# An attention backward kernel: K and V also read through a transposing DMA instead of being transposed on TensorE

## The chip, the cores and the metric

The kernel runs on one core of a Trainium2 chip. The metric is device time in microseconds (us), as the median of several executions. Engines are named as in the profile: PE is TensorE, PEld is TensorE loading the operand that a matmul holds still, DVE is VectorE, ACT is ScalarE, POOL is GpSimd, SP is SyncE, which computes nothing here and only issues DMAs. A q behind a name (SPq) is that engine's instruction queue. PSUM is the memory into which matmuls write in these kernels. The granted clock is the share of TensorE's full clock that the trace records: 1 or 0.5 at any moment here.

## The reference, cut to what matters

Two independent attention blocks (A and B) with batch 8, 96 queries, 32 heads, 512 cached keys, head size 128, model width 640, all bfloat16. The program returns the forward output and, for a given output gradient, the gradients of x, K, V, wq and wo:

```python
q = (x @ wq).reshape(B, Sq, H, Dh).transpose(0, 2, 1, 3)
scores = jnp.einsum("bhqd,bhkd->bhqk", q, k_cache) * (Dh ** -0.5)
p = softmax(scores)
o = jnp.einsum("bhqk,bhkd->bhqd", p, v_cache)
out = o.transpose(0, 2, 1, 3).reshape(B, Sq, H * Dh) @ wo      # then jax.vjp of it
```

One (block, head, batch) triple is a *cell*. There are 2 x 32 x 8 = 512 cells. Each needs K and V twice: with keys on the partitions (for dQ and O), as they lie in memory, and with the head dimension on the partitions (for the scores S and for dP), which is their transpose.

## The kernel before

A cell's work is cut into steps that are emitted tick by tick, so that several cells overlap. The parts that the change touches (cuts are marked with `# ...`):

```python
OFF = dict(ld=0, s1=2, s2=3, s3=3, s4=4, s5=5, s6=6, s7=7, s8=8)   # tick of each step

def c_ld(h, b):                       # natural K and V; partition p holds keys 4p..4p+3
    K_sb = kvp.tile([128, KC, 128], BF16, name="K_sb", bufs=11)
    V_sb = kvp.tile([128, KC, 128], BF16, name="V_sb", bufs=8)
    nc.sync.dma_start(K_sb[:], kc[b, h].rearrange("(p c) d -> p c d", c=KC))
    nc.sync.dma_start(V_sb[:], vc[b, h].rearrange("(p c) d -> p c d", c=KC))

def c_s1(h, b):                       # eight PE transposes into one PSUM bank, one DVE copy
    for c in range(KC):
        nc.tensor.transpose(kvT_ps[:, c * 128:(c + 1) * 128], st["K_sb"][:, c, :], ident[:])
    for c in range(KC):
        nc.tensor.transpose(kvT_ps[:, Sk + c * 128:Sk + (c + 1) * 128], st["V_sb"][:, c, :], ident[:])
    nc.vector.tensor_copy(KVT[:], kvT_ps[:])

def c_s2a(h, b):                      # scores: one matmul of 512 moving columns
    nc.tensor.matmul(S_ps[:], hs["QT_h"][:, tok], st["KT"], start=True, stop=True)
# ... softmax; P_sb scaled on POOL; O, dV, dP, dS, dQ ...
def c_s7(h, b):                       # dK: four matmuls, ACT copies out of PSUM, SP stores
    # ...
    dK_sb = wk.tile([128, KC * 128], BF16, name="dK_sb", bufs=3)
    nc.scalar.activation(dK_sb[:], dK_ps[:], ACT.Identity, scale=1.0)
    nc.sync.dma_start(dk[b, h].rearrange("(p c) d -> p (c d)", c=KC), dK_sb[:])
```

dV is stored the same way in step 4. Per head, wo and wq are also transposed on PE (ten transposes). SP issues four copies of 128 KB for each cell: K, V, dK, dV.

## Time and profile before

1850.55 us (median of two runs, 1850.18 to 1850.92).

| resource | busy of 1849 us |
|---|---|
| PE | 1818 (98%) |
| DVE / ACT / POOL | 1519 / 1434 / 778 |
| 16 DMA engines, mean packet time | 1071 (58%) |
| SP: its records plus the short gaps between them | 880 + 130 = 1010 (55%) |

A DMA queue's packet time is summed and divided by 16 engines. For SP, I add the durations of all its instructions and every gap of at most 150 ns between two of them: those short gaps recur after each instruction and are not waits.

From the page of the kernel before: the span, the busy times, the granted clock and DMA share in 40 slices of the span, the two DMA queues that matter (packets, MB, share), the chain that ended last, and two groups of instructions (count, total busy us, mean ns of one, then idle time just before them and what ended most of it):

```profile
span 1848.8 us, 69797 instructions
...
PE 1818.4 (98%) x26595; PEld 1571.4 (85%) x26744; DVE 1518.6 (82%) x3309; ACT 1434.4 (78%) x4041; POOL 777.9 (42%) x1378
...
PEclk9999999999999999999999999999999999999999
DMA  7666654666546655566575665456655566555652
...
q1 hardware_dynamic: 296480, 270.53, 46.2%
q0 software_dynamic: 19872, 60.32, 10.7%
...
PE 95%; POOL 2%; issue 1%; DVE 1%; DMA 1%; ACT 0%; POOLq 0%; SPq 0%; ACTq 0%
...
L396 ACT ACTIVATE dK_sb<-dK_ps 128x512 bf16<-128x512 f32 x512 | 300.5, 587 | 15.7 <-PE dK_ps L394 12.9
...
L259 PE MATMUL S_ps<-KVT,QT_h 128*96 128x512 bf16 x512 | 193.8, 379 | 2.2 <-DVE KVT L247 1.9
```

PE is full, the clock is fully granted, and the chain is 95% PE. The S matmul takes 379 ns and waits for almost nothing (2.2 us in all).

The SP queue in a stretch of the same trace; columns are start, duration, queue, line, operation:

```profile
901.18 0.34 SPq L397 DMA_DIRECT2D out_dram<-dK_sb  x1
902.18 0.34 SPq L333 DMA_DIRECT2D out_dram<-dV_sb  x1
903.09 0.34 SPq L233 DMA_DIRECT2D K_sb<-in_B_k_cache_dram  x1
903.66 1.38 SPq L234 DMA_DIRECT2D V_sb<-in_B_v_cache_dram  x1
```

A copy holds SP for 0.34 us, with free time between.

### The profile page before, as it was taken

The page shows a single profiled execution, that of the slowest core. Times are in us where ns is not written, and L with a number is a line of the kernel's source. Part 1 is how long each engine was busy: PE and PEld are TensorE (multiplying, and loading weights), DVE is VectorE, ACT ScalarE, POOL GpSimd, SP SyncE. Part 2 cuts the span into 40 slices and gives each one's busy share as a digit, 9 for nine tenths or more (in the row PEclk, how much of TensorE's full clock was granted, in tenths as well). Part 3 has the DMA queues.
Part 4 walks back from the last instruction along what each step waited for, and adds up shares of the span by engine and source line. Part 5 has one row for each costly group of instructions (what it writes and reads, how often), then busy time and mean ns, then how long its engine had stood idle before and what let it go on. Part 6 is the DMA issues. An engine that isn't in the chain of part 4 may idle for free.

```text
span 1848.8 us, 69797 instructions
## 1 busy us (share of the span) xinstructions
PE 1818.4 (98%) x26595; PEld 1571.4 (85%) x26744; DVE 1518.6 (82%) x3309; ACT 1434.4 (78%) x4041; POOL 777.9 (42%) x1378
## 2 busy tenths in 40 slices
PE   6999999999999999999999999999999999999998
PEld 5888888888888888888888888888888888888887
DVE  5888867888788887888878887678887888878885
ACT  4888877888668886788767888788876788767882
POOL 4444433444334443345455444334433444333435
PEclk9999999999999999999999999999999999999999
DMA  7666654666546655566575665456655566555652
GB/s 229 196 193 202 192 162 149 199 195 193 164 148 194 201 183 165 159 191 205 186 229 173 196 194 184 160 167 198 192 175 164 171 196 199 159 165 176 201 168 84
DMA packets 316688, 335.32 MB, mean 181 GB/s; under 512 B 38368, under 2 KB 302048, under 8 KB 316352
## 3 DMA queue, kind: packets, MB, share of 16 engines
q1 hardware_dynamic: 296480, 270.53, 46.2%
q0 software_dynamic: 19872, 60.32, 10.7%
q8 instruction: 210, 3.44, 0.8%
q14 instruction: 126, 1.03, 0.2%
HBM read 171.57 MB, written 159.12 MB: 179 GB/s over the span
## 4 chain that ended last, share of the span: by engine, by line
PE 95%; POOL 2%; issue 1%; DVE 1%; DMA 1%; ACT 0%; POOLq 0%; SPq 0%; ACTq 0%
PE q_ps L210 11%; PE o_ps L480 10%; PE dV_ps L330 6%; PE kvT_ps L243 6%; PE kvT_ps L245 6%; PE dK_ps L394 6%; PE dP_ps L352 6%; PE S_ps L259 6%; PE dwq_ps L445 6%; PE dwo_ps L425 5%; PE optp_ps L313 5%; PE dq_dst_ps L377 5%; PE optp_ps L306 5%; PE dq_dst_ps L370 5%; PE n_ps L225 3%; PE nat_ps L410 2%
## 5 line engine op out<-in xcount | busy, mean ns | idle before, releaser
L290 POOL TENSOR_SCALAR P_sb<-E_sb,rinv 96x512 bf16<-96x512 bf16 x512 | 354.2, 692 | 780.5 <-DVE rinv L281 775.2
L271 ACT ACTIVATE E_sb<-S_ps,negm 96x512 bf16<-96x512 f32 x512 | 349.1, 682 | 291.2 <-DVE negm L261 288.1
L356 DVE SCALAR_TENSOR_TENSOR dS_sb<-dP_ps,dl_ps,P_sb 96x512 bf16<-96x512 f32 x512 | 383.3, 749 | 108.1 <-PE dl_ps L354 103.1
L247 DVE COPY KVT<-kvT_ps 128x1024 bf16<-128x1024 bf16 x512 | 350.0, 684 | 70.7 <-PE kvT_ps L245 69.0
L261 DVE TENSOR_REDUCE negm<-S_ps 96x1 f32<-96x512 f32 x512 | 347.6, 679 | 35.8 <-PE S_ps L259 30.1
L332 ACT ACTIVATE dV_sb<-dV_ps 128x512 bf16<-128x512 f32 x512 | 313.3, 612 | 0.0
L396 ACT ACTIVATE dK_sb<-dK_ps 128x512 bf16<-128x512 f32 x512 | 300.5, 587 | 15.7 <-PE dK_ps L394 12.9
L319 ACT ACTIVATE PT_sb<-optp_ps 128x384 bf16<-128x384 bf16 x512 | 253.4, 495 | 0.0
L245 PE MATMUL kvT_ps<-ident,V_sb 128*128 128x128 bf16 x2048 | 198.0, 219 | 0.0
L394 PE MATMUL dK_ps<-Qnat_h,dS_sb 96*128 96x128 bf16 x2048 | 197.9, 219 | 0.0
L243 PE MATMUL kvT_ps<-ident,K_sb 128*128 128x128 bf16 x2048 | 197.9, 219 | 0.0
L330 PE MATMUL dV_ps<-dOnat_h,P_sb 96*128 96x128 bf16 x2048 | 197.9, 219 | 0.0
L259 PE MATMUL S_ps<-KVT,QT_h 128*96 128x512 bf16 x512 | 193.8, 379 | 2.2 <-DVE KVT L247 1.9
L352 PE MATMUL dP_ps<-KVT,dOT_h 128*96 128x512 bf16 x512 | 195.2, 381 | 0.0
L342 POOL TENSOR_TENSOR prod<-OT_h,dOT_h 128x96 bf16<-128x96 bf16 x512 | 186.2, 364 | 19.4 <-ACT OT_h L316 14.4
L243 PEld LDWEIGHTS <-K_sb 128*128 128x128 bf16 x2048 | 147.3, 98 | 36.9 <-issue 1.9
L379 DVE COPY dST_sb<-dq_dst_ps 128x384 bf16<-128x384 bf16 x512 | 175.4, 343 | 1.8 <-PE dq_dst_ps L377 0.8
L313 PE MATMUL optp_ps<-ident,P_sb 96*128 96x96 bf16 x2048 | 171.6, 205 | 2.3 <-POOL P_sb L290 2.0
L377 PE MATMUL dq_dst_ps<-ident,dS_sb 96*128 96x96 bf16 x2048 | 172.1, 206 | 0.5 <-DVE dS_sb L356 0.4
L306 PE MATMUL optp_ps<-PT_sb,V_sb 128*128 128x96 bf16 x2048 | 172.1, 206 | 0.0
L370 PE MATMUL dq_dst_ps<-dST_sb,K_sb 128*128 128x96 bf16 x2048 | 170.7, 206 | 0.0
L445 PE MATMUL dwq_ps<-dQnat,x_nat 128*128 128x128 bf16 x1920 | 143.2, 219 | 0.0
(84 smaller groups left out, 3949.8 us busy)
## 6 DMA issues: line engine op xcount, KB each, us to landing
out_dram<-dV_sb SPq DMA_DIRECT2D x512, 128.0 KB, 2.0
out_dram<-dK_sb SPq DMA_DIRECT2D x512, 128.0 KB, 2.3
K_sb<-in_A_k_cache_dram SPq DMA_DIRECT2D x256, 128.0 KB, 2.4
V_sb<-in_A_v_cache_dram SPq DMA_DIRECT2D x256, 128.0 KB, 2.5
K_sb<-in_B_k_cache_dram SPq DMA_DIRECT2D x256, 128.0 KB, 2.4
V_sb<-in_B_v_cache_dram SPq DMA_DIRECT2D x256, 128.0 KB, 2.5
out_dram<-dwq_sb POOLq DMA_DIRECT2D x64, 160.0 KB, 3.0
out_dram<-dwo_sb POOLq DMA_DIRECT2D x64, 160.0 KB, 2.7
```

The costliest lines, as they stand in the source:

```text
L243: nc.tensor.transpose(kvT_ps[:, c * 128:(c + 1) * 128], st["K_sb"][:, c, :], ident[:])
L245: nc.tensor.transpose(kvT_ps[:, Sk + c * 128:Sk + (c + 1) * 128], st["V_sb"][:, c, :], ident[:])
L247: nc.vector.tensor_copy(KVT[:], kvT_ps[:])
L259: nc.tensor.matmul(S_ps[:], hs["QT_h"][:, tok], st["KT"], start=True, stop=True)
L261: nc.vector.tensor_reduce(negm[:], S_ps[:], axis=AX.X, op=ALU.max, negate=True)
L271: nc.scalar.activation(E_sb[:], st["S_ps"][:], ACT.Exp, bias=st["negm"][:], scale=1.0, accum_out=rowsum[:])
L290: nc.gpsimd.tensor_scalar(P_sb[:], st["E_sb"][:], st["rinv"][:], 0.0, op0=ALU.mult, op1=ALU.add)
L330: nc.tensor.matmul(dV_ps[:, c * 128:(c + 1) * 128], P_sb[:, c * 128:(c + 1) * 128], hs["dOnat_h"][:, b * 128:(b + 1) * 128], start=True, s ...
L332: nc.scalar.activation(dV_sb[:], dV_ps[:], ACT.Identity, scale=1.0)
L352: nc.tensor.matmul(dP_ps[:], hs["dOT_h"][:, tok], st["VT"], start=True, stop=True)
L356: nc.vector.scalar_tensor_tensor(dS_sb[:], dP_ps[:], dl_ps[:, 0:1], st["P_sb"][:], op0=ALU.subtract, op1=ALU.mult)
L394: nc.tensor.matmul(dK_ps[:, c * 128:(c + 1) * 128], dS_sb[:, c * 128:(c + 1) * 128], hs["Qnat_h"][:, b * 128:(b + 1) * 128], start=True, s ...
```

## The change

The intent is to take the transposes off the full engine. K and V are read a second time by a DMA that transposes on the way, straight into the layout that S and dP need. Two heads' cells interleave so that one such DMA reads 16 rows of 16 KB (two heads, eight rows each). wo and wq are read transposed as well. The transposed tile holds keys in an order that a matmul reads in runs of eight (16 bytes), so the natural loads and the gradient stores have to use the same key order: partition f*8+r holds keys r*64+4f to r*64+4f+3.

```diff
-def c_ld(h, b):
-    nc.sync.dma_start(K_sb[:], kc[b, h].rearrange("(p c) d -> p c d", c=KC))
-    nc.sync.dma_start(V_sb[:], vc[b, h].rearrange("(p c) d -> p c d", c=KC))
-def c_s1(h, b):   # eight PE transposes, DVE copy
+R8 = 16 // HP                 # 8
+F4 = Sk // R8 // KC           # 16
+def keys_in(kv, h, b):
+    return kv[b, h].rearrange("(r f c) d -> f r (c d)", r=R8, f=F4, c=KC)
+
+def p_ldT(h, b, which):       # once for a pair of heads
+    t_ = kvp.tile([128, F4 * KC, 16], BF16, name=key + "_p", bufs=5)
+    src = (kc if which == 0 else vc)[b, h:h + HP].rearrange("h (r f) d -> (h r) (f d)", r=R8)
+    nc.sync.dma_start_transpose(t_[:], src)
+    for j in range(HP):
+        CS[...][key] = t_[:, :, j * R8:(j + 1) * R8].rearrange("p (f c) r -> p c f r", c=KC)
+
+def c_ldn(h, b, which):
+    # ... tile t_
+    nc.sync.dma_start(t_[:].rearrange("p c d -> p (c d)"), keys_in(kc if which == 0 else vc, h, b))
 # dV, and dK likewise:
-    nc.sync.dma_start(dv[b, h].rearrange("(p c) d -> p (c d)", c=KC), dV_sb[:])
+    nc.sync.dma_start(keys_in(dv, h, b), dV_sb[:])
 # OT leaves PSUM on DVE instead of ACT
-    nc.scalar.activation(hs["OT_h"][:, tok], OT_ps, ACT.Identity, scale=1.0)
+    nc.vector.tensor_copy(hs["OT_h"][:, tok], OT_ps)
 # weights: woT_p (a pair of heads) and wqT_r (a group of 4) by nc.sync.dma_start_transpose,
 # the ten PE transposes a head removed
# ... ticks of all steps, groups of 4 heads instead of 8, buffer counts ...
```

More of the change, by code (lines that the diff above doesn't have):

```diff
@@ L33 @@
 SL_S2B = 5.5
-SL_S1 = 6
 SL_S8 = 10
@@ L43 @@
 SL_SETUP = 96
-OFF = dict(ld=0, s1=2, s2=3, s3=3, s4=4, s5=5, s6=6, s7=7, s8=8)
-HK = dict(pA=-5, pB=-3, pC0=[-2, 0], pC1=[-1, 0], pD1=1, pD0=2, qA0=13, qA1=17, qB=[20, 17], qD=[(18, 0, 2), (19, 2, 5)])
-EV = dict(pB0="act", pB1="dve", pC00="act", pC01="act", pC10="act", pC11="dve", pD0="dve", pD1="dve", qA0="dve", qA1="dve", qB0="act", qB1="act", qD="dve", gU="act")
+OFF = dict(kt=-4, vt=-1, kn=3, vn=0, s2=3, s3=3, s4=4, s5=5, s6=6, s7=7, s8=8)
+HP = 2
+HK = [
+    dict(pA=-12, pB=-12, pC0=[-6, -4], pC1=[-5, -3], pD1=-2, pD0=0, qA0=21, qA1=25, qB=[28, 25], qD=[(26, 0, 2), (27, 2, 5)]),
+    dict(pA=-12, pB=-12, pC0=[-1, 3], pC1=[1, 2], pD1=3, pD0=5, qA0=29, qA1=33, qB=[36, 33], qD=[(34, 0, 2), (35, 2, 5)]),
+]
+EV = dict(pC00="act", pC01="act", pC10="act", pC11="dve", pD0="dve", pD1="dve", qA0="dve", qA1="dve", qB0="act", qB1="act", qD="dve", gU="act")
 GSPREAD0 = 9
@@ L50, with build_block @@
 GSPREAD1 = 9
-SLOTS = dict(LOAD=0, S2A=5, S2B=5.5, S1=6, S8=10, S7=20, S5=30, S4=40, S6=50, S3A=52, S3B=53, S5B=54, HEAD=SL_HEAD, GRP=SL_GRP)
-def build_block(tc, em, tick0, blk, x, kc, vc, wq, wo, g_all, out_all, dx, dk, dv, dwq, dwo, ident, ones, pools, HG=8, first=True, groups=None):
+SLOTS = dict(LOAD=0, S2A=5, S2B=5.5, S8=10, S7=20, S5=30, S4=40, S6=50, S3A=52, S3B=53, S5B=54, HEAD=SL_HEAD, GRP=SL_GRP)
+def build_block(tc, em, tick0, blk, x, kc, vc, wq, wo, g_all, out_all, dx, dk, dv, dwq, dwo, ident, ones, pools, HG=4, first=True, groups=None):
     nc = tc.nc
@@ L146, in build_block @@
         if not first:
-            em.add(tick0 - 8 + c - 2, SL_LOAD, setup_ld(0, c))
-            em.add(tick0 - 7 + c - 2, SL_LOAD, setup_ld(1, c))
-        em.add(tick0 - 8 + c, SL_SETUP, setup_T(0, c))
-        em.add(tick0 - 7 + c, SL_SETUP, setup_T(1, c))
-    em.add(tick0 + (-11 if first else B + OFF["s5"] - 2), SL_LOAD, setup_nat(1))
-    em.add(tick0 + (-12 if first else B + OFF["s8"] - 2), SL_LOAD, setup_nat(0))
+            em.add(tick0 - 12 + c - 2, SL_LOAD, setup_ld(0, c))
+            em.add(tick0 - 11 + c - 2, SL_LOAD, setup_ld(1, c))
+        em.add(tick0 - 12 + c, SL_SETUP, setup_T(0, c))
+        em.add(tick0 - 11 + c, SL_SETUP, setup_T(1, c))
+    em.add(tick0 + (-15 if first else 21), SL_LOAD, setup_nat(1))
+    em.add(tick0 + (-16 if first else 20), SL_LOAD, setup_nat(0))
     def evac(eng, dst, src, sc=None):
@@ L164, in f @@
         def f():
-            wo_h = hd.tile([128, D], BF16, name="wo_h", bufs=1)
-            nc.gpsimd.dma_start(wo_h[:], wo[h * 128:(h + 1) * 128, :])
-            wq_h = hd.tile([128, DC, 128], BF16, name="wq_h", bufs=1)
-            with nc.allow_non_contiguous_dma(reason="per-head wq slice"):
-                nc.gpsimd.dma_start(wq_h[:], wq_v[:, :, h * 128:(h + 1) * 128])
-            HS[(blk, h)] = dict(wo_h=wo_h, wq_h=wq_h)
+            wq_p = hd.tile([128, DC, HP * 128], BF16, name="wq_p", bufs=2)
+            with nc.allow_non_contiguous_dma(reason="per-pair wq slice"):
+                nc.gpsimd.dma_start(wq_p[:], wq_v[:, :, h * 128:(h + HP) * 128])
+            woT_p = hd.tile([128, DC, HP * 128], BF16, name="woT_p", bufs=2)
+            nc.sync.dma_start_transpose(woT_p[:], wo[h * 128:(h + HP) * 128, :])
+            for j in range(HP):
+                HS[(blk, h + j)] = dict(woT_h=woT_p[:, :, j * 128:(j + 1) * 128], wq_h=wq_p[:, :, j * 128:(j + 1) * 128])
         return f
@@ L175, in f @@
             st = HS[(blk, h)]
-            woT_ps = bank([128, DC * 128], BF16, "woT_ps")
-            for c in range(DC):
-                nc.tensor.transpose(woT_ps[:, c * 128:(c + 1) * 128], st["wo_h"][:, c * 128:(c + 1) * 128], ident[:])
-            woT_h = hd.tile([128, DC * 128], BF16, name="woT_h", bufs=1)
-            evac(EV["pB0"], woT_h[:], woT_ps[:])
-            st["woT_h"] = woT_h
-            wqT_ps = bank([128, DC * 128], BF16, "wqT_ps")
-            for c in range(DC):
-                nc.tensor.transpose(wqT_ps[:, c * 128:(c + 1) * 128], st["wq_h"][:, c, :], ident[:])
-            wqT_h = hst.tile([128, D], BF16, name="wqT_h")
-            evac(EV["pB1"], wqT_h[:], wqT_ps[:])
-            st["wqT_h"] = wqT_h
             st["OT_h"] = hst.tile([128, T], BF16, name="OT_h")
             st["dQT_h"] = hst.tile([128, T], BF16, name="dQT_h")
-            st["QT_h"] = hd.tile([128, T], BF16, name="QT_h")
-            st["dOT_h"] = hd.tile([128, T], BF16, name="dOT_h")
+            st["QT_h"] = hd.tile([128, T], BF16, name="QT_h", bufs=4)
+            st["dOT_h"] = hd.tile([128, T], BF16, name="dOT_h", bufs=4)
         return f
@@ L204, in f @@
                 dst = st["dOT_h"]
-                lhs = lambda c: st["woT_h"][:, c * 128:(c + 1) * 128]
+                lhs = lambda c: st["woT_h"][:, c, :]
                 rhsT = S["gT"]
@@ L217, in f @@
             src = st["QT_h"] if which == 0 else st["dOT_h"]
-            dst = hd.tile([Sq, B * 128], BF16, name="Qnat_h" if which == 0 else "dOnat_h")
+            dst = hd.tile([Sq, B * 128], BF16, name="Qnat_h" if which == 0 else "dOnat_h", bufs=4)
             st["Qnat_h" if which == 0 else "dOnat_h"] = dst
@@ L227, in pD @@
         return f
-    def c_ld(h, b):
-        def f():
-            K_sb = kvp.tile([128, KC, 128], BF16, name="K_sb", bufs=11)
-            V_sb = kvp.tile([128, KC, 128], BF16, name="V_sb", bufs=8)
-            nc.sync.dma_start(K_sb[:], kc[b, h].rearrange("(p c) d -> p c d", c=KC))
-            nc.sync.dma_start(V_sb[:], vc[b, h].rearrange("(p c) d -> p c d", c=KC))
-            CS[(blk, h, b)] = dict(K_sb=K_sb, V_sb=V_sb)
+    R8 = 16 // HP
[3 more added lines that the diff above has]
+    def p_ldT(h, b, which):
+        def f():
+            key = "KT" if which == 0 else "VT"
+            t_ = kvp.tile([128, F4 * KC, 16], BF16, name=key + "_p", bufs=5)
+            src = (kc if which == 0 else vc)[b, h:h + HP].rearrange("h (r f) d -> (h r) (f d)", r=R8)
+            nc.sync.dma_start_transpose(t_[:], src)
+            for j in range(HP):
+                CS.setdefault((blk, h + j, b), {})[key] = t_[:, :, j * R8:(j + 1) * R8].rearrange("p (f c) r -> p c f r", c=KC)
         return f
-    def c_s1(h, b):
+    def c_ldn(h, b, which):
         def f():
-            st = CS[(blk, h, b)]
-            kvT_ps = bank([128, 2 * Sk], BF16, "kvT_ps")
-            for c in range(KC):
-                nc.tensor.transpose(kvT_ps[:, c * 128:(c + 1) * 128], st["K_sb"][:, c, :], ident[:])
-            for c in range(KC):
-                nc.tensor.transpose(kvT_ps[:, Sk + c * 128:Sk + (c + 1) * 128], st["V_sb"][:, c, :], ident[:])
-            KVT = wk.tile([128, 2 * Sk], BF16, name="KVT", bufs=5)
-            nc.vector.tensor_copy(KVT[:], kvT_ps[:])
-            st["KT"] = KVT[:, 0:Sk]
-            st["VT"] = KVT[:, Sk:2 * Sk]
+            key = "K_sb" if which == 0 else "V_sb"
+            t_ = kvp.tile([128, KC, 128], BF16, name=key, bufs=7)
+            nc.sync.dma_start(t_[:].rearrange("p c d -> p (c d)"), keys_in(kc if which == 0 else vc, h, b))
+            CS[(blk, h, b)][key] = t_
         return f
@@ L396, in f @@
             nc.scalar.activation(dK_sb[:], dK_ps[:], ACT.Identity, scale=1.0)
-            nc.sync.dma_start(dk[b, h].rearrange("(p c) d -> p (c d)", c=KC), dK_sb[:])
+            nc.sync.dma_start(keys_in(dk, h, b), dK_sb[:])
         return f
@@ L435, in f @@
             dQnat = st["dQnat"]
-            if "dwq_sb" not in st:
-                st["dwq_sb"] = hd.tile([128, DC, 128], BF16, name="dwq_sb")
-                st["dwq_n"] = 0
-            dwq_sb = st["dwq_sb"]
+            pr = HS[(blk, h - h % HP)]
+            if "dwq_sb" not in pr:
+                pr["dwq_sb"] = hd.tile([128, DC, HP * 128], BF16, name="dwq_sb", bufs=1)
+                pr["dwq_n"] = 0
+            dwq_sb = pr["dwq_sb"]
+            j = h % HP
             ncn = c_hi - c_lo
@@ L446, in f @@
                                      start=(t == 0), stop=(t == TT - 1))
-            evac(EV["qD"], dwq_sb[:, c_lo:c_hi, :].rearrange("p a b -> p (a b)"), w_ps[:, 0:ncn * 128])
-            st["dwq_n"] += ncn
-            if st["dwq_n"] == DC:
-                with nc.allow_non_contiguous_dma(reason="per-head dwq slice"):
-                    nc.gpsimd.dma_start(dwq_v[:, :, h * 128:(h + 1) * 128], dwq_sb[:])
+            evac(EV["qD"], dwq_sb[:, c_lo:c_hi, j * 128:(j + 1) * 128], w_ps[:, 0:ncn * 128].rearrange("p (a b) -> p a b", b=128))
+            pr["dwq_n"] += ncn
+            if pr["dwq_n"] == DC * HP:
+                with nc.allow_non_contiguous_dma(reason="per-pair dwq slice"):
+                    nc.gpsimd.dma_start(dwq_v[:, :, (h - j) * 128:(h - j + HP) * 128], dwq_sb[:])
         return f
@@ L457, in f @@
             nc.gpsimd.dma_start(wo_r[:, 0:groups[g], :], wo[GH0[g] * 128:(GH0[g] + groups[g]) * 128, :].rearrange("(h p) d -> p h d", p=128))
-            G[g] = dict(wo_r=wo_r)
+            wqT_r = grp.tile([128, HG, D], BF16, name="wqT_r", bufs=1)
+            nc.sync.dma_start_transpose(wqT_r[:, 0:groups[g], :], wq[:, GH0[g] * 128:(GH0[g] + groups[g]) * 128])
+            G[g] = dict(wo_r=wo_r, wqT_r=wqT_r)
             if g == 0:
@@ L478, in f @@
                 src = HS[(blk, h)]["OT_h"] if which == 0 else HS[(blk, h)]["dQT_h"]
-                rhs = G[g]["wo_r"][:, hh, c0:c0 + w] if which == 0 else HS[(blk, h)]["wqT_h"][:, c0:c0 + w]
+                rhs = G[g]["wo_r"][:, hh, c0:c0 + w] if which == 0 else G[g]["wqT_r"][:, hh, c0:c0 + w]
                 nc.tensor.matmul(o_ps[:], src[:, t * 128:(t + 1) * 128], rhs, start=(hh == 0), stop=(hh == groups[g] - 1))
             if NG == 1:
-                ob = wk.tile([128, w], BF16, name="ob", bufs=6)
+                ob = wk.tile([128, w], BF16, name="ob", bufs=5)
                 evac(EV["gU"], ob[:], o_ps[:])
@@ L489, in f @@
             else:
-                ob = wk.tile([128, w], BF16, name="ob", bufs=6)
+                ob = wk.tile([128, w], BF16, name="ob", bufs=5)
                 nc.vector.tensor_tensor(ob[:], o_ps[:], acc[:, t, c0:c0 + w], op=ALU.add)
@@ L501, in build_block @@
             h = h0 + hh
-            c0t = tick0 + h * B
-            em.add(c0t + HK["pA"], SL_LOAD, pA(h))
-            em.add(c0t + HK["pB"], SL_HEAD, pB(h))
+            j = h % HP
+            c0t = tick0 + (h - j) * B
+            hk = HK[j]
+            if j == 0:
+                em.add(c0t + hk["pA"], SL_LOAD, pA(h))
+            em.add(c0t + hk["pB"], SL_HEAD, pB(h))
             for si in range(NTS):
-                em.add(c0t + HK["pC0"][min(si, len(HK["pC0"]) - 1)], SL_HEAD, pC(h, 0, si))
-                em.add(c0t + HK["pC1"][min(si, len(HK["pC1"]) - 1)], SL_HEAD, pC(h, 1, si))
-            em.add(c0t + HK["pD1"], SL_HEAD, pD(h, 1))
-            em.add(c0t + HK["pD0"], SL_HEAD, pD(h, 0))
+                em.add(c0t + hk["pC0"][min(si, len(hk["pC0"]) - 1)], SL_HEAD, pC(h, 0, si))
+                em.add(c0t + hk["pC1"][min(si, len(hk["pC1"]) - 1)], SL_HEAD, pC(h, 1, si))
+            em.add(c0t + hk["pD1"], SL_HEAD, pD(h, 1))
+            em.add(c0t + hk["pD0"], SL_HEAD, pD(h, 0))
             for b in range(B):
-                ct = c0t + b
-                em.add(ct + OFF["ld"], SLOTS["LOAD"], c_ld(h, b))
-                em.add(ct + OFF["s1"], SLOTS["S1"], c_s1(h, b))
+                ct = c0t + b * HP + j
+                if j == 0:
+                    em.add(ct + OFF["kt"], SLOTS["LOAD"], p_ldT(h, b, 0))
+                    em.add(ct + OFF["vt"], SLOTS["LOAD"], p_ldT(h, b, 1))
+                em.add(ct + OFF["kn"], SLOTS["LOAD"], c_ldn(h, b, 0))
+                em.add(ct + OFF["vn"], SLOTS["LOAD"], c_ldn(h, b, 1))
                 em.add(ct + OFF["s2"], SLOTS["S2A"], c_s2a(h, b))
@@ L526, in build_block @@
                 em.add(ct + OFF["s7"], SLOTS["S7"], c_s7(h, b))
-            em.add(c0t + HK["qA0"], SL_HEAD, qA(h, 0))
+            em.add(c0t + hk["qA0"], SL_HEAD, qA(h, 0))
             for di in range(len(dsplits)):
-                em.add(c0t + HK["qB"][min(di, len(HK["qB"]) - 1)], SL_HEAD + 1, qB(h, di))
-            em.add(c0t + HK["qA1"], SL_HEAD, qA(h, 1))
-            qd_parts = HK["qD"]
-            for (k_, c_lo, c_hi) in qd_parts:
+                em.add(c0t + hk["qB"][min(di, len(hk["qB"]) - 1)], SL_HEAD + 1, qB(h, di))
+            em.add(c0t + hk["qA1"], SL_HEAD, qA(h, 1))
+            for (k_, c_lo, c_hi) in hk["qD"]:
                 if c_lo < DC:
                     em.add(c0t + k_, SL_HEAD + 2, qD(h, c_lo, min(c_hi, DC)))
-        cLg = tick0 + (h0 + groups[g] - 1) * B + B - 1
+        cLg = tick0 + (h0 + groups[g]) * B - 1
         gs0 = max(3, (GSPREAD0 * groups[g]) // HG)
@@ L552, in _kernel_impl @@
 def _kernel_impl(tc, A_x, A_k_cache, A_v_cache, A_wq, A_wo, B_x, B_k_cache, B_v_cache, B_wq, B_wo, grad_out,
-           out_0, out_1, out_2, out_3, out_4, out_5, out_6, out_7, out_8, out_9, out_10, HG=8, slots=None, off=None, hk=None, ev=None, gspread=None, groupsA=None, groupsB=None):
+           out_0, out_1, out_2, out_3, out_4, out_5, out_6, out_7, out_8, out_9, out_10, HG=4, slots=None, off=None, hk=None, ev=None, gspread=None, groupsA=None, groupsB=None):
     global GSPREAD0, GSPREAD1
@@ L578, in _kernel_impl @@
             hd=P(name="hd", bufs=2),
-            hst=P(name="hst", bufs=HG + 2),
+            hst=P(name="hst", bufs=9),
             grp=P(name="grp", bufs=1),
-            stp=P(name="stp", bufs=6),
+            stp=P(name="stp", bufs=4),
         )
@@ L587, in _kernel_impl @@
         em = Emitter()
-        t_next = 13
+        t_next = 20
         for blk, args in enumerate(((A_x, A_k_cache, A_v_cache, A_wq, A_wo, grad_out, out_0, out_1, out_2, out_3, out_4, out_5),
```

## The prediction

> **What bounds the kernel now.** TensorE. The page of busy times gives PE 1818 us of 1849 (98%), DVE 82%, ACT 78%, POOL 42%; the chain of waits that ended last is 95% PE. The granted clock is 0.999 throughout, so nothing is throttled. The DMA engines are busy 58% on the mean (HW queue 46.2%, software queue 10.7%) and move 335 MB, so a full engine share is worth about 310 GB/s (181 / 0.58; the table of stretches gives 306 to 330).
>
> **What the change removes.** Per cell (512 of them) eight 128x128 PE transposes of K and V. The group list says 219 ns each, but they are pipelined: in the timeline four of them take a step of 0.22 to 0.23 us. So 0.45 us a cell, 230 us in all (the chain's 12% for these two lines agrees). The ten wo and wq transposes a head cost 0.057 us each, 36 us. PE work falls from 1818 to about 1552 us; with start and drain, a PE floor near 1585. All of this lies on the critical path. DVE loses the KVT copies (350 us) and wqT copies (30), and gains the OT copies from ACT: 96 columns from PSUM, estimated 0.24 us from DVE's 410 and 547 ns for 256 and 384 columns, so 125 us: DVE about 1265. ACT loses OT (126) and woT (47): about 1260. Both go to 80% of a 1585 span, so neither binds.
>
> **What it adds.** K and V are read twice: 512 transposing DMAs of 256 KB (134 MB), plus 21 MB for wo and wq; the wo loads that go are 10 MB. Total about 480 MB. The existing copies keep 1 KB pieces, so about 1048 us of all 16 engines at 310 GB/s (the natural loads now step 16 KB between pieces, so I hope for no gain there). For the transposes before has no record; the Trainium skill, "DMA: Bandwidth & Descriptors", section "Latency and other measured facts", gives 261 GB/s for strided ones and about 350 to 400 for contiguous ones. Rows of 16 KB should be at the better side of the middle; my estimate is 0.75 to 1.0 us each, 385 to 515 us, plus about 65 for weights. DMA demand: 1500 to 1625 us. So DMA becomes a second bound as high as PE. The SP queue issues all of them: four copies at 0.34 us a cell (timeline) plus one transpose of perhaps 1 us: 2.4 of about 3.1 us, in order.
>
> **Strided moving operand.** KT and VT are now read in runs of eight keys (16 bytes). The skill, "SBUF — State Buffer", Door 1, names 16-byte lines and full rate within one line, so S and dP matmuls should keep about 380 ns. No run of before shows this.
>
> **Prediction.** Two near-full resources with shared in-order issue do not overlap perfectly: 1655 us, range 1590 to 1770. Faster by over 2%: 0.86; within 2%: 0.08; slower: 0.06.
>
> **What would show it right.** kvT_ps, woT_ps, wqT_ps groups gone; PE busy near 1550 to 1600; DVE and ACT near 1260; DMA share 88 to 98%, about 285 GB/s; S and dP matmuls unchanged; PE idle of 30 to 120 us, waiting mainly for transposed tiles or natural K/V loads, with SP waits mostly gone.
>
> **What would make it wrong.** (1) Transposes run nearer 400 GB/s, or overlap with copies: then PE-bound, about 1590. (2) Transposes cost over 1.3 us of all engines, or each drains the queue: DMA or SP bound at 1750 to 1900. (3) 16-byte runs slow the moving read: S and dP groups longer than 380 ns, up to 200 us lost. (4) The strided natural loads and stores lose HBM efficiency: packet time per KB rises. (5) PE gaps lower the granted clock.

## The result

2336.2 us (median of two runs, 2334.71 to 2337.7): slower by a factor of 1.2621 (95% interval 1.2585 to 1.2658). Such ratios are the mean time of one kernel's fast runs over that of the other's in the same rounds, so not quite the ratio of the medians quoted here. Executions over 1.5% slower than the fastest of the same kernel are left out of the means. The result is correct.

From the page of the changed kernel, the lines that answer to those of before:

```profile
span 2335.8 us, 60652 instructions
...
PE 1815.0 (78%) x22008; PEld 1447.8 (62%) x22008; DVE 1392.1 (60%) x3533; ACT 1342.1 (57%) x3465; POOL 690.4 (30%) x1258
...
PEclk8898998998999999889898999999998989989998
DMA  9777877878787877778888887887888878877774
...
q1 hardware_dynamic: 404512, 425.79, 71.9%
q0 software_dynamic: 14880, 49.82, 6.9%
...
DMA 39%; PE 35%; ACT 13%; issue 5%; SPq 4%; DVE 3%; POOL 1%; ACTq 0%; POOLq 0%; DVEq 0%
...
L389 ACT ACTIVATE dK_sb<-dK_ps 128x512 bf16<-128x512 f32 x512 | 304.4, 594 | 590.2 <-DMA out_dram<-dK_sb 512.4
...
L252 PE MATMUL S_ps<-KT_p,QT_h 128*96 128x512 bf16 x512 | 213.1, 416 | 135.2 <-ACT dK_sb L389 117.0
```

No compute engine is full: PE is at 78%. The DMA engines are at 79%. The clock has fallen to a mean of 0.911: the trace records half clock for about 415 us. That is most of why PE is busy for 1815 us, as before, with a sixth fewer matmuls: at full clock it would be 1653 us by my estimate (1815 x 0.911). The chain is 39% DMA, but not the loads that I had expected: it is the *stores* of dK and dV (28 and 11%). ACT's dK copy now waits 590 us, 512 of them for a dK store to free its staging buffer, and the S matmul waits 117 us behind that ACT copy.

Why are stores late, with DMA engines at 79% and a landing time of 2.7 us against 2.0 to 2.3 before? Look at the queue that issues them. The SP queue of the changed kernel, same columns as before:

```profile
1103.36 1.19 SPq L232 DMA_TRANSPOSE VT_p<-in_A_v_cache_dram  x1
1104.64 0.60 SPq L390 DMA_DIRECT2D out_dram<-dK_sb  x1
1105.33 0.77 SPq L326 DMA_DIRECT2D out_dram<-dV_sb  x1
1106.19 1.23 SPq L232 DMA_TRANSPOSE KT_p<-in_A_k_cache_dram  x1
1107.51 0.59 SPq L241 DMA_DIRECT2D K_sb<-in_A_k_cache_dram  x1
1108.18 0.58 SPq L241 DMA_DIRECT2D V_sb<-in_A_v_cache_dram  x1
1108.85 0.59 SPq L390 DMA_DIRECT2D out_dram<-dK_sb  x1
1109.54 0.58 SPq L326 DMA_DIRECT2D out_dram<-dV_sb  x1
1110.21 0.59 SPq L241 DMA_DIRECT2D K_sb<-in_A_k_cache_dram  x1
1110.88 0.58 SPq L241 DMA_DIRECT2D V_sb<-in_A_v_cache_dram  x1
1111.55 1.19 SPq L232 DMA_TRANSPOSE VT_p<-in_A_v_cache_dram  x1
```

The queue is solid. From one V transpose to the next it took 8.19 us for two cells: two transposes at 1.2 us and eight copies at about 0.59. A copy holds SP for 0.58 to 0.60 us instead of 0.34. The statistics by line agree (count, then shortest / median / longest hold in ns, then first and last start). Of the kernel before, its K loads:

```profile
L233 SPq DMA_DIRECT2D K_sb<-in_A_k_cache_dram x256: 327/340/1863, 1.8 to 879.8; - x128
```

Of the changed kernel, block A's natural loads and its transposes:

```profile
L241 SPq DMA_DIRECT2D V_sb<-in_A_v_cache_dram x256: 536/577/2212, 20.0 to 1147.2; - x128
L241 SPq DMA_DIRECT2D K_sb<-in_A_k_cache_dram x256: 536/587/1890, 25.8 to 1159.3; - x128
```

```profile
L232 SPq DMA_TRANSPOSE KT_p<-in_A_k_cache_dram x128: 1115/1223/5842, 11.6 to 1122.3; - x128
L232 SPq DMA_TRANSPOSE VT_p<-in_A_v_cache_dram x128: 1122/1184/2770, 18.7 to 1140.6; - x128
```

Even the shortest copy (536 ns) is over the median of before (340), so the longer hold is not an effect of load alone. Summed over the trace, SP's records take 2101 us and the short gaps 189: 2290 of 2336 us, 98%. Only 46 us are left over for waits.

### The profile page after: what moved, and what is told of

Read it like the earlier page. It is cut to its first block, busy times and chain, and to the rows that moved or that the text cites. A ratio compares the mean times of both kernels' runs of the same rounds, so it can differ in the third digit from the quotient of the medians.

```text
span 2335.8 us, 60652 instructions
## 1 busy us (share of the span) xinstructions
PE 1815.0 (78%) x22008; PEld 1447.8 (62%) x22008; DVE 1392.1 (60%) x3533; ACT 1342.1 (57%) x3465; POOL 690.4 (30%) x1258
## 3 DMA queue, kind: packets, MB, share of 16 engines
HBM read 161.09 MB, written 159.12 MB: 137 GB/s over the span
## 4 chain that ended last, share of the span: by engine, by line
DMA 39%; PE 35%; ACT 13%; issue 5%; SPq 4%; DVE 3%; POOL 1%; ACTq 0%; POOLq 0%; DVEq 0%
DMA out_dram<-dK_sb 28%; DMA out_dram<-dV_sb 11%; PE q_ps L202 7%; ACT dK_sb L389 5%; PE o_ps L477 4%; PE S_ps L252 3%; ACT E_sb L264 3%; ACT dV_sb L325 3%; PE dwq_ps L440 2%; PE dwo_ps L418 2%; PE dK_ps L387 2%; PE dq_dst_ps L370 2%; PE dV_ps L323 2%; PE dq_dst_ps L363 2%; PE dP_ps L345 2%
## 5 line engine op out<-in xcount | busy, mean ns | idle before, releaser
L252 PE MATMUL S_ps<-KT_p,QT_h 128*96 128x512 bf16 x512 | 213.1, 416 | 135.2 <-ACT dK_sb L389 117.0
L274 DVE RECIPROCAL rinv<-rowsum 96x1 f32<-96x1 f32 x512 | 80.7, 158 | 392.6 <-ACT E_sb L264 380.3
L387 PE MATMUL dK_ps<-Qnat_h,dS_sb 96*128 96x128 bf16 x2048 | 216.0, 233 | 8.8 <-ACT dK_sb L389 5.7
L363 PE MATMUL dq_dst_ps<-dST_sb,K_sb 128*128 128x96 bf16 x2048 | 186.0, 218 | 39.9 <-ACT dK_sb L389 28.2
L323 PE MATMUL dV_ps<-dOnat_h,P_sb 96*128 96x128 bf16 x2048 | 213.3, 230 | 3.6 <-ACT dV_sb L325 3.3
L477 PE MATMUL o_ps<-wo_r,OT_h 128*128 128x256 bf16 (+1 forms) x1152 | 162.3, 265 | 66.8 <-ACT dK_sb L389 65.5
L345 PE MATMUL dP_ps<-VT_p,dOT_h 128*96 128x512 bf16 x512 | 209.5, 409 | 2.9 <-ACT dV_sb L325 2.3
L370 PE MATMUL dq_dst_ps<-ident,dS_sb 96*128 96x96 bf16 x2048 | 187.1, 218 | 22.8 <-DVE dS_sb L349 22.5
L477 PE MATMUL o_ps<-wqT_r,dQT_h 128*128 128x256 bf16 (+1 forms) x1152 | 165.2, 267 | 45.7 <-ACT dK_sb L389 45.0
L202 PE MATMUL q_ps<-xT,wq_p 128*128 128x512 bf16 (+1 forms) x640 | 147.0, 359 | 63.3 <-ACT dK_sb L389 62.1
```

The source lines that it names most:

```text
L202: nc.tensor.matmul(q_ps[:], lhs(c), rhsT[:, c, t0:t0 + w], start=(c == 0), stop=(c == DC - 1))
L323: nc.tensor.matmul(dV_ps[:, c * 128:(c + 1) * 128], P_sb[:, c * 128:(c + 1) * 128], hs["dOnat_h"][:, b * 128:(b + 1) * 128], start=True, s ...
L363: nc.tensor.matmul(dQT_ps, st["K_sb"][:, c, :], st["dST_sb"][:, c * Sq:(c + 1) * Sq], start=(c == 0), stop=(c == KC - 1))
L387: nc.tensor.matmul(dK_ps[:, c * 128:(c + 1) * 128], dS_sb[:, c * 128:(c + 1) * 128], hs["Qnat_h"][:, b * 128:(b + 1) * 128], start=True, s ...
L477: nc.tensor.matmul(o_ps[:], src[:, t * 128:(t + 1) * 128], rhs, start=(hh == 0), stop=(hh == groups[g] - 1))
```

## The experiments

My theory after reading the two traces, called Q: SP's in-order issue queue is full, and it is full because a copy with the permuted (three-dimensional) pattern holds it nearly twice as long, and because the transposes are issued there too. Rivals: D, the DMA engines themselves bind; M, the permuted order is slow in memory; L, stores are merely delayed by a transpose ahead of them, which more buffers would cover. The table is for reference; each run is told below. SP and DMA are sums over the profiled execution's records, in us and as a share of its span.

| run | time | ratio to before | SP | DMA | PE busy | clock |
|---|---|---|---|---|---|---|
| before | 1850.6 | 1 | 1010 (55%) | 1071 (58%) | 98% | 0.999 |
| the change | 2336.2 | 1.2621 | 2290 (98%) | 1856 (79%) | 78% | 0.911 |
| before_permuted | 1851.6 | 1.0003 | 1486 (80%) | 1117 (60%) | 98% | 0.999 |
| more_store_bufs | 2334.9 | 1.2618 | 2290 (98%) | 1854 (79%) | 78% | 0.902 |
| natural_order | 2297.8 | 1.2418 | 1913 (83%) | 1823 (79%) | 98% | 0.977 |
| plain_copies (wrong) | 2070.3 | 1.1188 | 2010 (97%) | 1917 (92%) | 83% | 0.938 |
| pool_loads | 1905.5 | 1.0295 | 1751 (92%) | 1902 (99.5%) | 88% | 0.946 |
| one_in_eight (wrong) | 1812.3 | 0.9784 | 1721 (95%) | 1321 (73%) | 91% | 0.973 |
| plain_second_read (wrong) | 1808.5 | 0.9806 | 1156 (64%) | 1640 (91%) | 91% | 0.972 |
| one_in_eight_pool (wrong) | 1740.9 | 0.9402 | 895 (51%) | 1311 (75%) | 93% | 0.984 |
| floor_bufs (wrong) | 1705.3 | 0.9222 | 902 (53%) | 1314 (77%) | 94% | 0.993 |
| weights_only | 1819.6 | 0.9831 | 1217 (67%) | 1186 (65%) | 98% | 1.000 |
| half_k | 1824.0 | 0.9858 | 1591 (88%) | 1618 (89%) | 94% | 0.988 |
| half_k_late | 1832.5 | 0.9867 | 1589 (88%) | 1605 (89%) | 95% | 0.991 |
| half_k_bufs | 1776.6 | 0.9601 | 1595 (90%) | 1624 (92%) | 96% | 0.996 |

### before_permuted: the copy pattern alone, in the kernel before

PE transposes whatever key order it is given, so this kernel is correct.

```diff
-nc.sync.dma_start(K_sb[:], kc[b, h].rearrange("(p c) d -> p c d", c=KC))
+nc.sync.dma_start(K_sb[:].rearrange("p c d -> p (c d)"), keys_in(kc, h, b))   # V, dV, dK likewise
```

> The kernel before with only the permuted copy pattern (PE transposes kept; result correct). Theory Q (the in-order SP issue queue is what binds the changed kernel, and the permuted pattern is part of its cost): each of the 2048 copies holds SP about 0.58 us instead of 0.34, SP's own issue time rises from 843 to about 1250 us, and because 1250 is far under 1850 the time stays within 1% of before. Rival M (the permuted order costs HBM or DMA-engine time): the mean time of a 1 KB packet rises by over 10% from 50.7 ns, the DMA share goes over 65%, and the time rises by over 2%.

It took 1851.6 us: no change. The K loads of this run, by the same statistics:

```profile
L236 SPq DMA_DIRECT2D K_sb<-in_A_k_cache_dram x256: 536/587/1828, 1.8 to 881.2; - x128
```

The hold is 587 ns, as in the changed kernel, with no transpose anywhere. The mean hold over all 2048 copies rose from 0.41 to 0.63 us (842 to 1300 us of issue). The mean 1 KB packet went from 50.7 to 53.7 ns, 6%, so rival M has only a small part of truth. The pattern's price is paid in issue time, and a kernel whose SP has room (80% here) does not feel it. Whether it is the third dimension or the changed order of the addresses that lengthens the hold, no run sets apart.

### more_store_bufs: more staging for the stores

Two fewer setup buffers (stp) make the room.

```diff
-dV_sb = wk.tile(..., name="dV_sb", bufs=3);  dK_sb = wk.tile(..., name="dK_sb", bufs=3);  stp bufs=4
+dV_sb = wk.tile(..., name="dV_sb", bufs=4);  dK_sb = wk.tile(..., name="dK_sb", bufs=5);  stp bufs=2
```

> The changed kernel with 5 dK and 4 dV staging buffers instead of 3 and 3 (two fewer setup buffers pay for it). Theory Q: throughput of SP binds, more buffers only lengthen the queue: within 1% of 2336 us, and ACT waits somewhere else or a little less. Rival L (stores are late because a transpose holds the queue for a moment, a latency that buffers would cover): the 512 us of ACT waits for dK stores fall by over half and the time falls by over 5%, under 2220 us.

2334.9 us: nothing. The two ACT groups of this run's page show what a fuller queue does to a wait:

```profile
L325 ACT ACTIVATE dV_sb<-dV_ps 128x512 bf16<-128x512 f32 x512 | 306.2, 598 | 719.6 <-DMA out_dram<-dV_sb 647.5
...
L389 ACT ACTIVATE dK_sb<-dK_ps 128x512 bf16<-128x512 f32 x512 | 303.8, 593 | 68.2 <-PE dK_ps L387 63.1
```

The 512 us of waiting for dK stores fell to almost nothing, as rival L had said, and came back whole at dV (125 became 648), although dV has one buffer more too. The time did not move and SP stands at 98% as before. So I read the wait that moves as a throughput limit seen from outside. L falls.

### pool_loads: the natural loads issued from another queue

```diff
-nc.sync.dma_start(t_[:].rearrange("p c d -> p (c d)"), keys_in(kc if which == 0 else vc, h, b))
+nc.gpsimd.dma_start(t_[:].rearrange("p c d -> p (c d)"), keys_in(kc if which == 0 else vc, h, b))
```

> The changed kernel with the 1024 natural K and V loads issued from the POOL queue instead of SP; same bytes, same patterns, same transposes. Theory Q: SP's work falls from about 2290 to about 1560 us, so the time falls to the next bound, the DMA engines' packet time (1856 us in the changed kernel): 1880 to 2000 us. Rival D (the DMA engines, slowed by the transposes, already bind at 2336): no gain, 2280 us or more. SP busy share would then fall with no gain in time.

1905.5 us, 431 us less than the change, with the same bytes, patterns and transposes. Only the issuing queue of half the copies was changed; that queue moves them in packets of 4 KB where SP's has 1 KB, at 427 us of 16 engines instead of 447, which is no gain of that size. From its page:

```profile
PE 1681.6 (88%) x21835; PEld 1379.9 (72%) x22008; DVE 1374.2 (72%) x3533; ACT 1318.6 (69%) x3465; POOL 1238.2 (65%) x2282
...
DMA  9999999999999999999999999999999999999993
...
q1 hardware_dynamic: 257056, 291.51, 67.8%
q0 software_dynamic: 64032, 184.11, 30.9%
```

Theory Q holds: with D, this could not have gained. And the next bound is exactly the one that the sum had named: the DMA engines are now busy in every slice (the queues' 67.8 and 30.9% and a little instruction traffic make 99.5%). SP came to 1751 us and not to the expected 1560: beside full DMA engines a K or V transpose held it 1.65 us on the mean instead of 1.32. The Trainium skill, "DMA: Bandwidth & Descriptors", section "Issuing engines are not separate DMA queues", says that issuing from several engines only saves the sequencer's issue time, "which is usually small relative to the DMA itself". The first half agrees; here the second half does not: in the changed kernel a copy held SP for 0.615 us on the mean and took 0.44 us of the 16 engines, and the saving was worth 431 us.

### natural_order: the cheap copy pattern, paid for by the matmuls

```diff
 def keys_in(kv, h, b):
-    return kv[b, h].rearrange("(r f c) d -> f r (c d)", r=R8, f=F4, c=KC)
+    return kv[b, h].rearrange("(p c) d -> p (c d)", c=KC)
-    ... t_[:, :, j * R8:(j + 1) * R8].rearrange("p (f c) r -> p c f r", c=KC)
+    ... t_[:, :, j * R8:(j + 1) * R8].rearrange("p (f c) r -> p c r f", c=KC)
```

> The changed kernel with the copies back in the two-dimensional key order of before, and the S and dP matmuls reading the transposed tiles with a step of 128 bytes instead of runs of 16 bytes (result correct). Theory Q: copies 0.34 us again, SP falls by 2048 x 0.24 = 490 us to about 1800, time 1870 to 1980, unless the strided moving read is slow; then S and dP groups lengthen from about 410 ns. Rival D: bytes and packets are the same, so 2280 us or more.

2297.8 us. The time looks like rival D's, but the profile does not. From its page:

```profile
PE 2238.8 (98%) x21835; PEld 1353.1 (59%) x22008; DVE 1430.6 (62%) x3533; ACT 1332.1 (58%) x3465; POOL 689.2 (30%) x1258
...
L345 PE MATMUL dP_ps<-VT_p,dOT_h 128*96 128x512 bf16 x512 | 523.8, 1023 | 0.0
L252 PE MATMUL S_ps<-KT_p,QT_h 128*96 128x512 bf16 x512 | 522.4, 1020 | 0.8 <-DMA K_sb<-in_B_k_cache_dram 0.8
```

SP fell to 1913 us (83%), as Q said, and PE became full: S and dP take 1020 ns instead of 380. Twice 512 matmuls at 0.64 us more are 655 us. So the run exchanged one bound for another; its time alone would have misled. It also shows why the change chose its order: in the changed kernel S takes 416 ns at a clock of 0.911, which is 379 at full clock (416 x 0.911), and 380 in half_k_bufs below. Runs of 16 bytes cost nothing here, steps of 128 bytes 2.7 times. The Trainium skill, "SBUF — State Buffer", section "Door 1: The DMA port swizzle", says that accesses within one 16-byte line run at full bandwidth and each new line costs; both halves agree.

### plain_copies: the pattern alone, in the changed kernel

The matmuls keep their runs of 16 bytes, so keys no longer match between K and its transpose and the gradients are wrong.

```diff
-    return kv[b, h].rearrange("(r f c) d -> f r (c d)", r=R8, f=F4, c=KC)
+    return kv[b, h].rearrange("(p c) d -> p (c d)", c=KC)
```

> Wrong result on purpose (keys of the natural copies and of the transposed tiles no longer match): the changed kernel with only the pattern of its 2048 natural copies put back to the two-dimensional one; queue, bytes, transposes and matmuls untouched. Theory Q: SP's own work falls from 2100 to about 1730 us plus 190 us of fixed gaps, so about the same as the DMA engines' 1850: time 1880 to 1980 us, and PE's S and dP stay near 400 ns (the natural_order run lost its gain to strided moving reads of 1020 ns, not to SP). Rival D (transposes hold the queue whatever the copies cost): 2200 us or more.

2070.3 us. A gain of 266 us from the pattern alone, but I had expected 1880 to 1980. Block A's V loads:

```profile
L241 SPq DMA_DIRECT2D V_sb<-in_A_v_cache_dram x256: 334/403/1742, 19.8 to 1019.5; - x128
```

SP is still the full one: 1820 + 189 us of 2076, 97%. The mean hold of a copy fell from 0.615 to 0.479 us, not to the 0.411 of the kernel before: 2048 x 0.136 is 279 us, about the gain. Most of what is left goes with the place in the queue. Of the 2048 copies, 57 came after a pause of SP and held it 339 ns (median), 1459 right behind another copy (383), and 532 right behind a transpose (530). In the kernel before, with DMA at 58%, the first two were 343 and 382. So a transpose also lengthens the hold of the two-dimensional copy behind it; by an estimate from the means of these groups, this makes up 0.05 of the 0.07 us, and fuller DMA engines (92%) can account for the rest at most. The permuted copies of the changed kernel show no such order: 582, 580 and 591 ns. So the pattern is a bit more than half of the excess over 1851 (266 of 486 us), and not all of it.

### one_in_eight: the transposes taken away

One tile for each pair of heads serves all eight batches; results are wrong. This run and the next but one were made to see what is left without seven of eight K and V transposes. It ran after one_in_eight_pool, which is told below and which its expectation calls "that run"; U and V are two readings of that run.

```diff
-    t_ = kvp.tile(...); nc.sync.dma_start_transpose(t_[:], src)
+    if b == 0:
+        t_ = kvp.tile(...); nc.sync.dma_start_transpose(t_[:], src); HS[(blk, h, key)] = t_
+    t_ = HS[(blk, h, key)]
```

> Wrong result on purpose: one of eight transposes kept, as in one_in_eight_pool, but the natural loads stay on SP. That run ended at 1741, not 1600 to 1670, with PE idle 122 us. If POOL, which there also issues 1024 loads in order between its P and prod work, delays PE (reading U), it falls to 1640 to 1700 us here, PE waits for P_sb and dS shrink, SP about 1470 us plus 190 of gaps. If the interleaved schedule itself loses the time (reading V), it stays at 1720 to 1760 us with the same PE waits.

1812.3 us, outside both ranges that I had written. The records say why: the copies held SP for 0.638 us each on the mean, so SP came to 1560 + 161 = 1721 us, 95% of the span. Even with nearly all transposes gone, the permuted copies and weight transposes alone fill SP to almost the time of the kernel before. The run therefore says nothing on the two readings that it was meant for (U and V); I read it as one more case of Q.

### plain_second_read: same bytes, no transposition

Based on pool_loads; the tile's content is wrong.

```diff
-src = ...[b, h:h + HP].rearrange("h (r f) d -> (h r) (f d)", r=R8);  nc.sync.dma_start_transpose(t_[:], src)
+src = ...[b, h:h + HP].rearrange("h (p k) d -> (h p) (k d)", k=8);   nc.sync.dma_start(t_[:]..., src)
```

> Wrong result on purpose: pool_loads with each K and V transpose replaced by a plain copy of the same 256 KB into the same tile. Theory T (the transpose itself is slow on the DMA engines: 680 us of 16 engines for 134 MB, 197 GB/s): the second read costs about 350 to 420 us instead, the DMA total falls from 1902 to about 1600 us, time 1620 to 1740 us. Rival B (it is the doubled bytes, whatever their form): DMA share stays near 100%, time 1860 us or more.

1808.5 us (1804 to 1830). From its page:

```profile
PE 1640.6 (91%) x21835; PEld 1349.3 (75%) x22008; DVE 1367.2 (76%) x3533; ACT 1315.0 (73%) x3465; POOL 1234.6 (68%) x2282
...
q1 hardware_dynamic: 306208, 291.48, 56.7%
q0 software_dynamic: 64032, 184.11, 33.3%
...
HBM read 295.31 MB, written 159.12 MB: 252 GB/s over the span
```

The second read of 134 MB now costs 423 us of 16 engines (65,536 packets of 2 KB); as transposes it cost 680 us in pool_loads (8192 packets of 16 KB at 1.33 us each) and 619 us in the changed kernel. That is 317 GB/s against 197 to 217. DMA fell to 1640 us, as expected, and rival B is out; but the time missed its range by 68 us, with neither PE nor DMA full (91% each). What held the last 68 us was not tested. The last line also teaches how to read the page: its HBM bytes read are 134 MB more here than the 161.09 MB of the kernel with transposes, though both read the same bytes. That counter does not contain what transposing DMAs read: it stays at 161.09 MB in one_in_eight_pool too, where seven of eight K and V transposes are gone.

### one_in_eight_pool and floor_bufs: what PE alone would have taken

The first joins one_in_eight and pool_loads; the second adds five dK and five dV buffers (three of each transposed tile instead of five). Both are wrong.

> Wrong result on purpose: natural loads from POOL as in pool_loads, and only one of eight K and V transposes kept (the pair's first tile serves all eight batches). With SP and DMA both relieved (SP about 900 us, DMA about 1310), only the PE floor of the prediction, 1585 us, should be left: 1600 to 1670 us. If the time stays over 1750, something other than SP, DMA and PE binds the new schedule (a chain of waits among PE, ACT, DVE and POOL), and the PE floor was wrong too.

> Wrong result on purpose: one_in_eight_pool (SP and DMA relieved, 1741 us) with 5 dK and 5 dV staging buffers instead of 3. In half_k these buffers gave about 50 us, the store latency there being what was left. If the same latency makes up the 1741: 1670 to 1710 us, and the PE floor of 1585 was about right with only the waits among the engines left out. If it stays at 1730 to 1750, stores are not it, and PE's waits for P_sb and dS (about 50 us in that trace) and the lower clock of 0.984 (about 26 us) are what the floor lacked.

They took 1740.9 and 1705.3 us. In the first, I had expected 1600 to 1670: with SP at 51% and DMA at 75%, the schedule itself left PE idle for 122 us. Buffers gave 36 us of that, inside the range that I wrote for late stores. In floor_bufs PE is busy 1605 us (94%), and its longest waits are (total us, times, longest):

```profile
PE dq_dst_ps L373 <- DVE dS_sb L352: 25.1, 27, 1.5
PE optp_ps L309 <- POOL P_sb L286: 21.2, 25, 2.0
PE tp_ps L130 <- DMA g_nat<-in_grad_out_dram: 7.3, 1, 7.3
PE tp_ps L130 <- DMA x_nat<-in_A_x_dram: 6.0, 1, 6.0
```

About 46 us are waits for dS and P, 13 are the start. So the PE work of the prediction (1552 us at full clock) was some 40 us too low (an estimate: 1605 x 0.993 = 1594), and the 33 us that it allowed for PE's idle time too few: PE is idle for 97 us here. Together the floor of 1585 was 120 us too low in this schedule. What part of the rest comes from POOL, which issues 1024 loads here between its P steps, stays open.

### weights_only: one part of the change alone

The kernel before, with wo and wq transposed by DMA; K and V stay on PE.

```diff
-nc.gpsimd.dma_start(wo_h[:], wo[h * 128:(h + 1) * 128, :])
+nc.sync.dma_start_transpose(woT_h[:], wo[h * 128:(h + 1) * 128, :])
-# ten PE transposes and two copies out of PSUM
+nc.sync.dma_start_transpose(wqT_r[:, 0:groups[g], :], wq[:, GH0[g] * 128:(GH0[g] + groups[g]) * 128])
```

> The kernel before with only wo and wq transposed by DMA (result correct), one part of the change alone. PE loses ten transposes a head, 36 us of its 1818; SP has slack (843 us of issue plus about 130), DMA has slack (58%). PE still binds: 1805 to 1830 us. If the transposes delay the copies behind them on SP enough to stall PE, it is 1850 or more.

1819.6 us: 31 us less than before, where the 36 us of PE work had been expected to go. The mechanism works where SP and DMA have room.

### half_k, half_k_late and half_k_bufs: a version that beats both

K alone comes through the transposing DMA; V is transposed on PE again; POOL issues K's natural loads; OT goes back to ACT.

```diff
-OFF = dict(kt=-4, vt=-1, kn=3, vn=0, ...)
+OFF = dict(kt=-4, kn=3, vn=0, v1=3, ...)
-nc.sync.dma_start(t_[:]..., keys_in(...))
+(nc.gpsimd if which == 0 else nc.sync).dma_start(t_[:]..., keys_in(...))
-em.add(ct + OFF["vt"], SLOTS["LOAD"], p_ldT(h, b, 1))
+em.add(ct + OFF["v1"], 6, c_v1(h, b))        # four PE transposes of V_sb, one DVE copy to VT (bufs=5)
# half_k_late: kn=5
# half_k_bufs: kn=5, and dK_sb and dV_sb with bufs=5 instead of 3
```

> A version made to beat both (result correct): K by transposing DMA as in the changed kernel, V transposed by PE again, K's natural loads from POOL, V's from SP, the OT copy back on ACT. From the measured terms: PE floor 1585 + 115 = 1700 us, DMA about 1560 us, SP about 1530 us, so PE should bind at 1715 to 1790 us, under both 1851 and 1905. If DMA contention or the schedule eats it: 1800 us or more.

> half_k with K's natural load placed two ticks later, so that POOL no longer waits in order for its buffer (434 us of POOL waits there). Reading U: 1770 to 1800 us. If POOL's waits cost nothing: 1810 to 1835 us as half_k.

> half_k_late with 5 dK and 5 dV staging buffers instead of 3, in the space that the V transposed tiles left. Here SP is not full (about 1600 of 1816), so late stores are a latency that buffers can cover, unlike in the changed kernel: 10 to 40 us less than half_k_late. If nothing changes, stores were not what held PE.

half_k took 1824.0 us (1816 to 1834), over the range that I had hoped for. half_k_late took 1832.5 (fast runs 1812 to 1834): no gain, and POOL's waits for that buffer stayed at 435 us, so moving the load by two ticks did not even change them; a miss. half_k_bufs took 1776.6 (1771 to 1778), 4.0% under the kernel before (0.9585 to 0.9617). From its page:

```profile
PE 1700.1 (96%) x23868; PEld 1436.2 (81%) x24056; DVE 1442.8 (82%) x3533; ACT 1380.6 (78%) x3977; POOL 962.3 (54%) x1770
...
DMA  9989999999999889999989989999989999998983
...
PE 77%; DVE 6%; DMA 6%; issue 5%; ACT 2%; POOL 2%; ACTq 0%; SPq 0%; POOLq 0%; DVEq 0%
```

Here more buffers did help, by 34 to 63 us against half_k_late from run to run, more than the 10 to 40 expected, while in the changed kernel they did nothing. The difference that I see is whether the queue behind them has room: SP is at 90% here and was at 98% there.

## Why the prediction was wrong

- **The step that failed**: "four copies at 0.34 us a cell (timeline) plus one transpose of perhaps 1 us: 2.4 of about 3.1 us, in order." The 0.34 us was read from a copy with a two-dimensional pattern and carried over to one with a three-dimensional pattern. (It was also a typical copy and not the mean: over the 2048 copies of the kernel before that is 0.41.) I asked what the new order does to HBM ("so I hope for no gain there") and not what it does to the issuing queue. Measured in the change: copies 0.615 us on the mean, transposes 1.32, and 189 us of short gaps that I had left out; with the weights' transposes (126 us), 2290 us, or 4.5 us a cell against the 2.4 of the prediction. So SP's queue alone was longer than the whole predicted time, and it set the pace, not PE or DMA. before_permuted showed the copies' part by itself, pool_loads showed that SP was what bound, more_store_bufs that it was not a latency.
- My own list of errors named it only in passing: "(2) Transposes cost over 1.3 us of all engines, or each drains the queue: DMA or SP bound at 1750 to 1900". It blamed the transposes; plain_copies puts the copies' pattern at a bit more than half of the loss.
- **A second term was mis-sized too**: the transposes. I took 0.75 to 1.0 us each from the Trainium skill, "DMA: Bandwidth & Descriptors", section "Latency and other measured facts" (261 GB/s strided, about 350 to 400 contiguous). In the change each took 1.21 us of all 16 engines (217 GB/s), in pool_loads 1.33 (197), and the weights' took 131 us, not 65, so the DMA demand was 1856 to 1902 us and not 1500 to 1625. By itself this term would have made the change no faster than before: pool_loads is DMA-bound at 1905.
- **Right**: PE was the bound before. The transposes on PE were worth nearly what was said: 36 us expected and 31 measured for the weights, 230 expected and an estimated 192 for K and V (PE's busy time at full clock: 1786 in weights_only, 1594 in floor_bufs). kvT_ps, woT_ps and wqT_ps are gone. DVE was predicted near 1265 us and is 1392, ACT 1260 and is 1342: both too low, neither binding. On DVE I had overlooked that groups of four heads instead of eight mean three times as many additions into the output accumulators (144 became 432): 54 us became 156. OT on DVE takes 248 ns, estimated 240. The 16-byte runs read at full rate.
- **Wrong in its reading of signs**: PE was to be busy for 1550 to 1600 us and was for 1815, at the lower clock. PE was to wait "mainly for transposed tiles or natural K/V loads". It waited for ACT, which waited for stores. Once SP is full, everything behind it in order is late, and what showed first was a tile with the fewest buffers (dK and dV with 3; dV with 4 in more_store_bufs).
- **The clock** fell to 0.911, as item (5) had allowed. The Trainium skill, "TensorE: Matmul & The Clock Gate", section "Why this matters for your kernels", asks for no idle gaps over about 3 us between bursts. In the change's trace this agrees in part: PE has 36 gaps of over 3 us, and 33 of them are followed by half clock within 7 us, but 42 of the 81 falls to half clock have no gap so long in the 13 us before them. half_k_bufs, 96% busy with 3 such gaps, has 0.996. natural_order, 98% busy with no gap over 1.6 us after its start, still has about 100 us at half clock (0.977). So idle gaps are not the whole cause, and the rest stays open.

## What to carry to other kernels

Moving work off a full engine can move it onto a queue: add up the issue time of the DMA queue, instruction by instruction, before adding to it, and use a hold that was measured for that very access pattern. The Trainium skill, "Perfetto Trace Analysis", section 'What "DMA-bound" means', lists the sequencer of the issuing engine as a bound of its own, recognizable by a solid row of DMA slices; the queue at 98% beside DMA engines at 79% is that case. When a wait only moves to another place as its buffer grows, as in more_store_bufs, look for a full queue behind it, and when one change relieves it, sum up the next resource first (here DMA at 1856 us) to know where the gain will stop.

## What the Trainium skill lacked or had wrong

- "DMA: Bandwidth & Descriptors" lacks how long a trn2 DMA holds its issuing queue by access pattern (what it gives per instruction makes no such difference): a 128 KB copy of 128 rows of 1 KB held SP for 340 ns (median, after a pause; 383 behind a copy, 530 behind a transpose) with a two-dimensional DRAM pattern and for 576 to 591 with a three-dimensional one, and a 256 KB transpose for 1184 to 1223.
- The same page, section "Issuing engines are not separate DMA queues", calls the issue time usually small relative to the DMA: here a copy held SP for 0.615 us and took 0.44 us of 16 engines, issue was 98% of the span, and moving 1024 copies to another queue took 2336 us to 1905.
- "Advanced Engine Details and Errata", section "X-Bar Transpose (TRN2)", says that transposing DMAs are as fast as regular ones and expects 350 to 400 GB/s: 134 MB took 619 to 713 us of 16 engines as transposes (188 to 217 GB/s in the change, pool_loads and plain_copies) and 423 us as plain 2 KB copies (317 GB/s).
- "SBUF — State Buffer" states the 16-byte lines without a number for a matmul's moving operand: 512 columns took 380 ns in runs of 16 bytes and 1020 ns at a step of 128 bytes.
- No page says that the profile's HBM bytes read leave out what transposing DMAs read: 161.09 MB with transposes against 295.31 MB with plain copies of the same bytes.
